# mLSTM cell and leaky-ReLU block: q of the second chunk's steps in own buffer parts, asked for sooner, and copied out of PSUM by VectorE

## Chip, cores and metric

The kernel runs on one core of a Trainium2 chip. The metric is device time in microseconds, the median of several executions.

## What is computed

Two blocks follow each other. The first is an mLSTM cell over 4 batches, 8 heads, 768 time steps and a head dimension of 40; the second a matmul, a leaky ReLU and a matmul over the 3072 tokens that come out. Cut to what matters:

```python
for t in range(S):
    m_new = np.maximum(f_gate[:, :, t] + m, i_gate[:, :, t])
    f_stab = np.exp(f_gate[:, :, t] + m - m_new)
    i_stab = np.exp(i_gate[:, :, t] - m_new)
    C = f_stab * C + i_stab * einsum('bhd,bhe->bhde', vt, kt)
    n = f_stab * n + i_stab * kt
    h = einsum('bhde,bhe->bhd', C, qt)
    y[:, :, t] = sigmoid(o_gate[:, :, t]) * h / np.maximum(np.abs(n @ qt), 1.0)
x = y.transpose(0, 2, 1, 3).reshape(B * S, H * D)      # 3072 x 320
h = x @ w_in                                           # 320 x 2048
out = np.maximum(0.01 * h, h) @ w_out                  # 2048 x 320
```

## The kernel before

**Steps and chunks.** Time is cut into 6 chunks of 128 (`NB`), and a chunk has one step per batch, so there are 24 steps; step s is chunk `s // 4`, batch `s % 4`. `B` is 4. Within a step the cell is worked out in parallel over its 128 times: scores of k against q, weighted by exponentials of the gates, times v, plus the state that the step inherits. Steps 0 to 3 (first chunk) are written out by hand in `first_chunk`. Steps 4 to 7 (second chunk) transpose k and q on TensorE; steps from 8 on load k and q in blocks of 32 and transpose them on VectorE (`prep_kq`). The feed-forward block of a chunk (`ff_units`) runs beside the cell steps of the next one: matmuls `ph` with w_in (L790), leaky ReLU on ScalarE (L798), matmuls `po` with w_out (L825), a copy (L833) and the store.

**Buffers for q.** `rb_t` holds `NR` = 2 buffers of three parts each: part 0 is for k in blocks (from step 8 on), part 1 for q, part 2 for the output gate. `natural(s, i)` (L396) gives part i of buffer `s % 2` for the steps 4 to 7. Part 0 of both buffers is not used by these four steps, whose k goes to `kn`. So q of steps 4 and 6 share one place, and q of 5 and 7 the other.

**A step of the second chunk.** `u_split(s)` (L554) transposes k and q of the step, 8 heads, two halves of 64 times: 64 small matmuls against the identity into two PSUM banks `tk`, each of which gets one half's k on some partitions and q on others. Four copies (L570) then take them to `kqT` in SBUF, k of both halves first, then q of both. `prep_qs(s)` (L512) has GpSimd scale q by a gate into a tile named `y`. `u_parts(s)` (L628) first transposes that scaled q on TensorE into two banks `tq` (L550), copied by ScalarE (L552); then come the scores (L644) and the state's increments (L649), and VectorE multiplies scores and exponentials (L654). `u_plain(s)` (L686) makes `hN` from them (L695), the denominators and the gated output x; `u_x(s)` (L763) transposes x into `xT`, the input of the next chunk's feed-forward matmuls, by five copies per step on ScalarE (L775 to L779). `prep_exp` (L481) makes the exponentials on ScalarE (L488), after GpSimd has added the mask (`prep_mask`, L479). `gates(c)` prepares the gates of a chunk on VectorE.

**Weights.** They arrive as 64-bit numbers and are narrowed on the core: `load_weights(n)` fetches a block, `narrow_weights(n)` yields six instructions, three on ScalarE (L243, L245, L251) and three on VectorE (L247, L253, L257). There are 4 blocks of w_in and 8 of w_out. The narrowing of two w_in blocks and of all w_out blocks lies among the cell steps of the second chunk. `fetch` says at which unit of the loop the later w_out blocks are asked for; the last one (7) at unit 15.

**Order.** For TensorE, VectorE, ScalarE and GpSimd the order of the instructions is the order in which the code gives them (`manual_schedule`, L989), and each engine works strictly in its order. SyncE issues nearly all transfers into one queue; its order is not written out but set by the framework's scheduler when the kernel is built, from the order of the code and from what each transfer depends on. `ahead(s)` (L868) prepares a step: `u_split`, the exponentials, `prep_qs`, and the requests for k and q of step s + 2; `feed(s)` (L890) asks for k and v of a step and for the spread gates `w` (L437). In the second chunk the loop at L1016 runs the feed-forward units of the first chunk one by one, and puts cell units behind those whose numbers `place` lists.

Of the kernel before, what the change touches and what calls it, by code (L numbers as in the profile page):

```python
# [21 lines left out]
def kernel(  # L22
# [26 lines left out]
    nc = tc.nc  # L49
    B, H, S, D = q.shape  # L50
# [12 lines left out]
    SL = P // 2  # L63
# [57 lines left out]
    NR = 2  # L121
# [5 lines left out]
    rb_t = [consts.tile([P, 3, RW], F32, name=f"rb{n}") for n in range(NR)]  # L127
# [57 lines left out]
    def run_of(r, at):  # L185

        ks = SLOTS[r][at:]
        return ks[0], next((i for i in range(1, len(ks)) if ks[i] != ks[i - 1] + 2), len(ks))

    def load_weights(n, halves=(0, 1)):  # L190

        m = n - QN
        if n < QN:
            dst = w_in[:, n, :]
        else:
            dst = w_out[:, 2 * m : 2 * m + 2, :].rearrange("p a d -> p (a d)")
        to = dst
        if wide:
            if n < 2:
                at = NF * GT - 2 * WC * (n + 1)  # L200
                raw = acts_l[:, at : at + 2 * WC].bitcast(U64)
            elif n < QN:
                raw = raw_t[:, WC * (n - 2) : WC * (n - 1)]
            elif m < 2:
                raw = w_out[:].rearrange("p f d -> p (f d)")[:, (2 + m) * WC : (3 + m) * WC].bitcast(U64)
            else:
                at = (4, 0, 1, 2, 3, 4)[m - 2] * HW
                raw = raw_t[:, at : at + HW]
            raws[n] = (raw, dst)
            to = raw  # L210
        if n < QN:
            src = moe_w_in[:, n * QC : (n + 1) * QC].rearrange("(k p) (r c) -> r p k c", p=DP, r=2)
            by_slot = to.rearrange("p (k c) -> p k c", k=KC)
            by_half = to.rearrange("p (e k c) -> p e k c", e=2, c=P)
            for r in halves:
                at = 0
                while at < KC:
                    k0, many = run_of(r, at)
                    rows, ks = slice(DP * r, DP * (r + 1)), slice(k0, k0 + 2 * many - 1, 2)
                    eng = nc.gpsimd if r and n < 3 else nc.sync  # L220
                    if wide or n > 1:
                        eng.dma_start(by_slot[rows, at : at + many, :], src[r, :, ks, :])
                    else:
                        for e in range(2):
                            eng.dma_start(by_half[rows, e, at : at + many, :], src[r, :, ks, e * P : (e + 1) * P])
                    at += many
        else:
            rows = moe_w_out[2 * m * P : 2 * (m + 1) * P, :]
            nc.sync.dma_start(to.rearrange("p (a d) -> p a d", d=Dm), rows.rearrange("(a p) d -> p a d", p=P))
# [165 lines left out]

    def natural(s, i):  # L396

        t = rb_t[s % NR][:, i]
        return t[:, : H * D].rearrange("p (h d) -> p h d", d=D)

    def load_late(s, i):

        if B <= s < 2 * B:
            if i > 0:
                c, b = divmod(s, B)
                nc.sync.dma_start(natural(s, i), (k, q, o_gate)[i][b, :, ts(c, P), :].rearrange("h p d -> p h d"))
        elif s < NS:
            load_blocks(s, i)
# [145 lines left out]
    def u_split(s):  # L554

        d = st[s]
        d["kqT"] = wk.tile([P, 2, PR * P], F32, name="kqT")
        src = (d["k"], natural(s, 1))
        bank = [psc.tile([P, H, SL], F32, name=f"tk{r}", tag="c") for r in range(2)]
        for h in range(H):  # L560
            for i in range(2):
                for u, toks, rows in subs(s):
                    out_rows = rows if i == 0 else slice(SL * u, SL * u + D)
                    nc.tensor.matmul(  # L564
                        bank[u][out_rows, h, :], lhsT=src[i][toks, h, :D], rhs=ident[toks, toks], start=True, stop=True,
                    )
        for i in range(2):
            for u, toks, rows in subs(s):
                out_rows = rows if i == 0 else slice(SL * u, SL * u + D)
                nc.scalar.copy(d["kqT"][rows, i].rearrange("p (h t) -> p h t", t=SL), bank[u][out_rows])  # L570

    def u_transpose(s, copy=nc.scalar.copy):
        d = st[s]
# [294 lines left out]
    def ahead(s):  # L868

        if s < NS:  # L870
            if s < 2 * B:
                u_split(s)
            if s >= 2 * B:
                late[s] = 3
            lazy[s] = prep_exp(s)
            if s < 2 * B:
                prep_qs(s)
            else:
                prep_kq(s)
            if s + NR < NS:  # L880
                load_late(s + NR, 0)
                load_late(s + NR, 1)
                if s + NR >= 2 * B:
                    spread_q(s + NR)
            state_next(s, 0)
            prep_vu(s)
            if s + 1 <= 2 * B:
                prep_mask(s + 1)

    def feed(s):  # L890
        load(s)
        spread(s)
# [96 lines left out]
    with tc.manual_schedule(engines={E.PE, E.DVE, E.Activation, E.Pool}):  # L989
        ffs, part = first_chunk()  # L990
        for s in (B, B + 1):
            load_late(s, 1)
            feed(s)
            load_late(s, 2)
            load_weights(s - B + 2)
        for n in range(3):
            load_weights(QN + n)
        for s in (B + 2, B + 3):
            feed(s)


        ffs = ffs[2:]
        fetch = {5: (3, 4), 8: (5, 6), 15: (7,)}
        place = (2, 5, 7, 10, 12, 15, 16, 18, 21, 22, 24, 26, 28)
        late = {}
        masks = {0: (2, 3), 12: (4, 5)}
        pairs = (2, 2, 6, 6, 14, 14, 19, 19, 19)
        now = (None for n in range(2, QN + NF // 2) for _ in narrow_weights(n))
        for c in range(1, NB + 1):
            if c > 1:  # L1010
                ffs = ff_units(c - 1)
            cells = cell_units(c) if c < NB else []
            n_ff, n_c = len(ffs), len(cells)
            done = fed = 0
            waiting = []
            for i in range(n_ff):  # L1016
                if c == 1:
                    run(now, (0, 0, 0, 3, 3, 0)[i] if i < 6 else 3 if i < 14 else 4)
                    for n in fetch.get(i, ()):
                        load_weights(QN + n)  # L1020
                for s, steps in lazy.items():
                    if s in late and late[s] > 0:
                        late[s] -= 1
                    else:
                        run(steps, 3)
                for n in masks.get(i, ()) if 1 < c < NB else ():
                    if c * B + n < NS:
                        prep_mask(c * B + n)
                ffs[i]()
                if c == 1 and i == 0:  # L1030
                    run(part)
                    prep_mask(B)
                    ahead(B)
                    load_fi(3)
                if c + 1 < NB:
                    if i == (1 if c == 1 else 0):
                        gates(c + 1)
                    if i == (3 if c == 1 else 2):
                        gates_exp(c + 1)
                upto = min(n_c, sum(p <= i for p in (place if c == 1 else pairs)))  # L1040
                while done < upto:
                    fn, s = cells[done]
                    fn(s)
                    done += 1
                    if fn is u_mix:
                        waiting.append(s)
                    if fn is u_plain and s < 2 * B - 1 or fn is u_parts and s == 2 * B - 1:
                        ahead(s + 1)
                    elif fn is u_mix:
                        ahead(s + 2)  # L1050
                    elif fn is u_plain:
                        prep_mask(s + 2)
                        ahead(s + 2)
                if i >= n_ff // 2 - 1:
                    for s in waiting:
                        gather_x(s)
                    waiting.clear()
                while fed < done:
                    fn, s = cells[fed]
                    fed += 1  # L1060
                    if fn in (u_mix, u_plain):
                        load_late(s + NR, 2)
                        if s + NL < NS:
                            feed(s + NL)
# [31 lines left out]
```

## Time and profile before

| | |
|---|---|
| median of 3 runs | 527.08 us (526.78 to 527.77) |
| the profiled execution's own time | 524.4 us |
| its span | 522.5 us |
| TensorE busy | 509.1 us (97%) |
| VectorE, ScalarE, GpSimd busy | 205.3, 187.6, 106.9 us |
| moved by DMA | 59.12 MB, mean 113 GB/s |

The profiled execution is one run under the hardware profiler; times of single instructions below are from it, counted from the start of its span. A row of a timeline gives start, duration, engine, line, operation, tiles and shapes; brackets give the idle time just before and what ended it. SPq is SyncE's row of transfers: its duration is that of the issue, not of the transfer. The copies of L570 are 16, of 577 to 583 ns, the first at 47.5 and the last at 101.2 us.

### The profile page before, as it was taken

What the parts mean: (1) busy time and instruction counts of PE and PEld (TensorE: products, weight loads), DVE (VectorE), ACT (ScalarE), POOL (GpSimd) and SP (SyncE); (2) the same over time, 40 slices, a digit from 0 to 9 for tenths busy, and PEclk for the clock granted to TensorE, in tenths of its full rate; (3) what the DMA queues carried; (4) which work ended last, traced back from release to release, by engine and by line L of the source; (5) the groups of instructions that cost most, each with busy time, mean ns of one, the idle gap of its engine ahead of it and who ended that gap; (6) DMA issues with size and microseconds to landing.
All of it is one profiled execution on the core that took longest, in us unless ns stands there. A gap on an engine that the chain in (4) does not pass through costs nothing.

```text
span 522.5 us, 11302 instructions
## 1 busy us (share of the span) xinstructions
PE 509.1 (97%) x4507; PEld 331.1 (63%) x4507; DVE 205.3 (39%) x400; ACT 187.6 (36%) x477; POOL 106.9 (20%) x149
## 2 busy tenths in 40 slices
PE   8989987999999999999999999999999999999997
PEld 6878876777554677554677554677554677544674
DVE  6666453767048264048264038253037240000000
ACT  5559896858425122125112125112125100122100
POOL 4363313424015031016021016021013010000000
PEclk9889999999999999999999999999999999999999
DMA  9999875989646535665536665625532112000000
GB/s 122 137 206 156 180 188 145 220 196 169 159 92 135 127 80 148 141 140 125 123 93 155 139 140 116 134 82 157 136 77 71 44 40 87 14 0 1 13 13 25
DMA packets 164419, 59.12 MB, mean 113 GB/s; under 512 B 128432, under 2 KB 155632, under 8 KB 164368
## 3 DMA queue, kind: packets, MB, share of 16 engines
q1 hardware_dynamic: 163408, 56.31, 50.1%
q0 software_dynamic: 576, 1.97, 2.0%
q8 instruction: 35, 0.57, 0.5%
q10 hardware_dynamic: 384, 0.13, 0.1%
q14 instruction: 16, 0.13, 0.1%
HBM read 51.68 MB, written 6.70 MB: 112 GB/s over the span
## 4 chain that ended last, share of the span: by engine, by line
PE 89%; SPq 5%; DMA 2%; ACT 2%; issue 1%; DVE 1%; ACTq 0%; DVEq 0%
PE po L825 40%; PE ph L790 39%; SPq L378 3%; PE pT L725 3%; PE sd L644 3%; DMA acts<-in_moe_w_in_dram 1%; PE sd L649 1%; PE tk L564 1%; PE hN L695 1%; DMA rb<-in_q_dram 1%; PE tq L550 1%; SPq L383 0%; SPq L392 0%; ACT kqT L570 0%; PE tg L357 0%
## 5 line engine op out<-in xcount | busy, mean ns | idle before, releaser
L790 PE MATMUL ph<-xT,w_in 64*128 64x512 f32 (+1 forms) x1120 | 216.5, 537 | 3.5 <-ACT acts L798 1.9
L825 PE MATMUL po<-w_out,acts 128*128 128x320 f32 x768 | 211.1, 434 | 0.0
L825 PEld LDWEIGHTS po<-w_out,acts 128*128 128x128 f32 x768 | 144.5, 190 | 62.6 <-issue 3.8
L790 PEld LDWEIGHTS ph<-xT,w_in 64*128 64x128 f32 x1120 | 108.6, 189 | 97.5 <-issue 87.7
L798 ACT ACTIVATE acts<-ph 128x512 f32<-128x512 f32 (+1 forms) x112 | 53.6, 531 | 141.5 <-PE ph L790 141.5
L654 DVE TENSOR_TENSOR qn<-w,sd 64x512 f32<-64x512 f32 x40 | 27.4, 684 | 106.7 <-PE sd L649 58.6
L479 POOL TENSOR_TENSOR w<-w,i 128x512 f32<-128x512 f32 x20 | 27.3, 1375 | 126.0 <-DMA w<-a_dr 74.0
L622 POOL TENSOR_TENSOR S<-S,f 40x336 f32<-40x336 f32 x36 | 28.0, 779 | 102.1 <-PE pT L725 65.2
L488 ACT ACTIVATE w<-w,gT 128x64 f32<-128x64 f32 x160 | 41.2, 338 | 0.0
L833 ACT COPY y<-po 128x320 f32<-128x320 f32 x12 | 5.1, 422 | 83.2 <-PE po L825 83.2
L833 ACT COPY hn<-po 128x320 f32<-128x320 f32 x12 | 5.1, 425 | 75.7 <-PE po L825 75.7
L541 DVE TENSOR_TENSOR qn<-kqT,ea 64x512 f32<-64x512 f32 x32 | 26.9, 840 | 0.9
L732 DVE STREAM_TRANSPOSE hb<-pT 128x512 f32<-128x512 f32 x16 | 11.4, 714 | 39.2 <-PE pT L725 39.0
L739 POOL TENSOR_TENSOR xb<-xb,den 128x320 f32<-128x320 f32 x16 | 11.6, 727 | 67.1 <-DVE xb L736 67.1
L644 PEld LDWEIGHTS sd<-kqT 40*64 40x64 f32 x640 | 19.9, 135 | 6.1 <-issue 6.1
L644 PE MATMUL sd<-kqT 40*64 40x64 f32 x640 | 21.6, 220 | 0.0
L535 DVE STREAM_TRANSPOSE kqT<-rb 128x512 f32<-128x512 f32 x32 | 20.7, 686 | 1.2 <-DMA rb<-in_q_dram 1.1
L743 DVE STREAM_TRANSPOSE x<-xb 128x512 f32<-128x512 f32 x16 | 18.1, 1132 | 7.7 <-POOL xb L739 7.7
L649 PE MATMUL sd<-S,vu 64*40 64x42 f32 x576 | 20.2, 214 | 0.7 <-issue 0.7
L649 PEld LDWEIGHTS sd<-S,vu 64*40 64x40 f32 x576 | 18.6, 111 | 0.9 <-issue 0.9
L626 DVE TENSOR_TENSOR S<-S,sd 40x336 f32<-40x336 f32 x36 | 18.1, 503 | 1.0
L725 PEld LDWEIGHTS pT<-qn,S 128*64 128x64 f32 x512 | 15.6, 138 | 3.6 <-issue 3.5
(138 smaller groups left out, 348.9 us busy)
## 6 DMA issues: line engine op xcount, KB each, us to landing
w<-a_dr SPq DMA_DIRECT2D x40, 128.0 KB
rb<-in_k_dram SPq DMA_DIRECT2D x64, 80.0 KB
rb<-in_q_dram SPq DMA_DIRECT2D x64, 80.0 KB
rb<-in_o_gate_dram SPq DMA_DIRECT2D x64, 80.0 KB
ea<-a_dr SPq DMA_DIRECT2D x32, 128.0 KB
kn<-in_k_dram SPq DMA_DIRECT2D x24, 160.0 KB
raw<-in_moe_w_out_dram SPq DMA_DIRECT2D x6, 640.0 KB
S<-in_v_dram SPq DMA_DIRECT2D x80, 40.0 KB
```

The source lines that it names most:

```text
L479: nc.gpsimd.tensor_tensor(w, w, cm2.unsqueeze(1).to_broadcast([P, H, SL]), op=ALU.add)
L488: yield nc.scalar.activation(w[:, h, :], of, AF.Exp, bias=gT[c][:, 0, bh : bh + 1], scale=1.0)
L535: nc.vector.transpose(d["kqT"][:, i].rearrange("p (h t n) -> p h n t", n=TS, t=QW), raw_blocks(s, i, QW).rearrange("p (h n) d -> p h n d", ...
L541: nc.vector.tensor_tensor(mixed(s)[rows, 1 - r], d["kqT"][rows, 1].rearrange("p (h t) -> p h t", t=SL), d["ea"][rows], op=ALU.mult,)
L622: nc.gpsimd.tensor_tensor(new, old, g, op=ALU.mult)
L644: nc.tensor.matmul(bank[1 - u][toks, h, :], lhsT=kqT[rows, 0, ts(h, SL)], rhs=kqT[rows, 1, ts(h, SL)], start=True, stop=True,)
L649: nc.tensor.matmul(dC[u][:, h].rearrange("p k d -> p (k d)"), lhsT=d["ku"][toks, h], rhs=S_v[s % NL][toks, u, h, :, :V1], start=True, stop ...
L654: nc.vector.tensor_tensor(mixed(s)[toks, u], w[toks], bank[1 - u][toks], op=ALU.mult)
L725: nc.tensor.matmul(pT[DP * r : DP * (r + 1), j * P + u * SL : j * P + (u + 1) * SL], lhsT=S[:, u, h, :], rhs=m[:, u, h, :], start=True, st ...
L790: nc.tensor.matmul(ph[r][:, cols], lhsT=w_row(r, slot, j), rhs=xT[DP * r : DP * (r + 1), slot, cols], start=(slot == 0), stop=(slot == KC ...
L798: nc.scalar.activation(acts[:, f, cols], ph[r][:, cols], AF.Prelu, alpha=0.01)
L825: nc.tensor.matmul(po[n][:], lhsT=acts[:, f, ts(n, P)], rhs=w_out[:, f, :], start=(f == 0), stop=(f == NF - 1),)
```

## The change

Three things change, all for steps 4 to 7.

1. `natural(s, 1)` gives part 0 of the buffer for steps 4 and 5, and part 1 as before for steps 6 and 7. Each of the four steps then has its own place for q. Part 0 is next written by k in blocks of steps 8 and 9.
2. `ahead(4)` and `ahead(5)` no longer ask for q of steps 6 and 7. These are asked for ahead of the loop: q of step 6 before the first three w_out blocks, q of step 7 between the two feeds of steps 6 and 7.
3. In `u_split` the two q copies out of PSUM go to VectorE; the two k copies stay on ScalarE.

```diff
     def natural(s, i):
 
-        t = rb_t[s % NR][:, i]
+        t = rb_t[s % NR][:, 0 if i == 1 and s < B + NR else i]
...
                 out_rows = rows if i == 0 else slice(SL * u, SL * u + D)
-                nc.scalar.copy(d["kqT"][rows, i].rearrange("p (h t) -> p h t", t=SL), bank[u][out_rows])
+                (nc.vector.tensor_copy if i else nc.scalar.copy)(
+                    d["kqT"][rows, i].rearrange("p (h t) -> p h t", t=SL), bank[u][out_rows],
+                )
...
                 load_late(s + NR, 0)
-                load_late(s + NR, 1)
+                if s + NR >= 2 * B:
+                    load_late(s + NR, 1)
...
             load_late(s, 2)
             load_weights(s - B + 2)
+        load_late(B + 2, 1)
         for n in range(3):
             load_weights(QN + n)
-        for s in (B + 2, B + 3):
-            feed(s)
-
+        feed(B + 2)
+        load_late(B + 3, 1)
+        feed(B + 3)
```

## Prediction

> **What bounds the kernel now.** I read the busy slices of the page first, then the table of waits, then the timelines of the engines around the waits that concern q. The slices:
>
> ```profile
> span 522.5 us, 11302 instructions
> PE   8989987999999999999999999999999999999997
> ACT  5559896858425122125112125112125100122100
> ```
>
> One slice is 13.1 us. TensorE is full from slice 7 on (from about 91 us), so what it is given earlier there can shorten the run. Its idle time lies before: in slice 6 (78 to 91 us) both TensorE and ScalarE dip. The waits name it:
>
> ```profile
> PE tk L564 <- DMA rb<-in_q_dram: 2.9, 1, 2.9
> POOL y L517 <- DMA rb<-in_q_dram: 1.3, 1, 1.3
> ```
>
> tk is the transposing of `u_split`, y the scaled q of `prep_qs`; one step waits for its q. TensorE's timeline says which, and SyncE's why:
>
> ```profile
> 79.56 0.31 PE L564 MATMUL tk<-ident,kn 64*40 64x64 f32 x4
> 82.75 0.25 PE L564 MATMUL tk<-ident,rb 64*40 64x64 f32 x2 [2.88 <-DMA rb<-in_q_dram]
> ```
> ```profile
> 58.84 1.12 SPq L229 DMA_DIRECT2D w_out<-in_moe_w_out_dram  x2
> 61.02 11.76 SPq L383 DMA_DIRECT2D S<-in_v_dram  x4
> 79.62 0.53 SPq L406 DMA_DIRECT2D rb<-in_q_dram  x1
> 114.45 0.54 SPq L229 DMA_DIRECT2D raw<-in_moe_w_out_dram  x1
> ```
>
> This is step 6 (third of the second chunk). Its q is issued at 79.62, behind everything that SyncE fetched for steps 6 and 7, and lands 3.1 us later. Four v issues take 11.76 us, where four elsewhere take about 2.5: they stand in a full queue. The DMA share is 0.89 from 58 to 75 us.
>
> ScalarE sets the pace up to there, and is itself held by transfers twice:
>
> ```profile
> 62.24 2.37 ACT L570 COPY kqT<-tk 40x512 f32<-40x512 f32 x4 [0.88 <-PE tk L564]
> 65.13 1.38 ACT L243 ACTIVATE w_in<-raw 128x1280 f32<-128x1280 f32 x1 [0.53 <-DMA raw<-in_moe_w_in_dram]
> 119.87 0.79 ACT L243 ACTIVATE w_out<-raw 128x640 f32<-128x640 f32 x1 [8.13 <-DMA raw<-in_moe_w_out_dram]
> 132.88 0.42 ACT L833 COPY hn<-po 128x320 f32<-128x320 f32 x1 [0.54 <-PE po L825]
> 133.21 0.37 ACT L775 COPY xT<-xt 128x256 f32<-128x256 f32 x1
> ```
>
> Remember 119.87: the last weight block arrives there, and from there ScalarE works without a pause to 132.34. At the seam between the chunks the weight load of the next matmuls was waiting for ScalarE too:
>
> ```profile
> PEld ph L790 <- ACT xT L779: 0.4, 1, 0.4
> ```
> ```profile
> 133.17 2.16 PE po L825 x8
> 135.33 4.91 PE ph L790 x21
> ```
>
> [...]
>
> **The change, part by part.**
>
> *q of step 6 asked for sooner.* Steps 4 and 5 now read q from part 0 of their buffers, so steps 6 and 7 own part 1, and their q has nothing to wait for. In the built program SyncE issues q of step 6 straight behind the four loads of the last w_in block (the last begins at 58.19), before the w_out blocks. That w_in block lands at 65.1 (ScalarE starts on it at 65.13). A q is 160 KB in runs of 160 bytes. The k of step 6, of the same form, landed at 72.0, after the last w_out block before it had come nearly whole at 70.1 (arrivals of the DMA semaphores in the trace): some 1.0 to 1.9 us; I take 1.2. So q is there at about 66.5, 13 us before it is read. The step's transposing took 79.56 to 83.84, 4.28 us; step 7's took 1.12. Gain on TensorE: 4.28 - 1.12 = 3.16 us.
>
> *Does TensorE get to 79.56 sooner?* No. Before it stand ScalarE's activations, and these run on from 65.13 without a pause to 79.9. All that the change takes off ScalarE before that (steps 4 and 5, 2.3 us, with it TensorE's 0.75 us wait at 57.40) ends in a longer wait for that w_in block. Credit: 0.
>
> *q of step 7 asked for sooner.* Issued at 94.33, it landed at 98.23, and TensorE read it at 98.24: no wait, and no slack. With TensorE 3.16 us ahead it would have become a wait of about 3 us. Now it is issued before k of step 7, around 76 us. Worth nothing by itself, it keeps the gain.
>
> *The q copies on VectorE.* 8 copies leave ScalarE, each 0.580 us: 4.6 us. Nearest row for VectorE: L581, 128x512 out of PSUM, 0.671 us: 8 x 0.67 = 5.4 us, on an engine 39% busy. The end of a step's copies: before, 4 x 0.58 = 2.32 us after tk; now 0.58 + 0.58 + 0.67 = 1.83 us, since the second bank's k copy goes first. Between 1.83 and 2.6 us (all in series with hand-overs) nobody is late: scores are 4.5 us of ph matmuls or more behind tk. VectorE's waiting copy blocks what is queued behind it, mostly weight narrowing (L253, L257); in step 6 that is wanted by po at 92.68 - 3.2 = 89.5 and would be done by about 84. In step 4 `gates` starts 1.3 us later and ends at 53.2, before the scores' product (54.27 before, then limited by ScalarE at about 53.1). At nothing; without that cover at most 0.6 us a step.
>
> *The DMA queue.* No transfer is added. q of step 6 pushes the three w_out blocks, and k, v and w of step 6, back by about 1.2 us, q of step 7 those of step 7 by 0.6 more. First use: w_out at 73.87, in by 66.6 before, so 67.8 now. w of step 6: POOL's mask (L479) began at 76.88, as w came; now about 78.1, over at 79.4, in time for POOL's next work at 79.76. Later two issues (0.6 us each) are missing from the row, at 79.62 and 94.33[...]. So the last weight block, issued at 114.45, should come within -0.6 to +0.8 us of 119.85; I take 0 and call the shift D.
>
> *What is late next.* All of SyncE's waits between 61 and 119 us on compute are under 1.3 us, so an earlier TensorE doesn't bring that block sooner. Thus ScalarE starts on it at 119.87 + D as before, and its row of work is unchanged: 12.47 us without a pause to 132.34, then the hn copy (0.33 to the next start; its wait of 0.54 is gone, po being early), then the first xT copy of step 7 (0.35): 133.02 + D. TensorE, 3.16 ahead, ends po at 135.33 - 3.16 = 132.17, and its next matmuls need that copy. In the built program the first waits for the copies up to L777 (the changed kernel's number) alone, the slots after for the rest, which come sooner than they are reached. So the second chunk's ph begins at 133.02 + D against 135.33: **2.3 us sooner**, 0.85 us of the gain turned into a new wait there. po's last quarter needs the block narrowed: 123.43 + D against 126.05 + 1.07 - 3.16 = 123.96, just in time.
>
> From there TensorE is full to the end and the shift stays. Sum: 3.16 - 0.85 = 2.3. The profiled execution: 524.4 (span 522.5 and 1.9 around it) to 522.1. The median of the runs shown, 527.08, stands 2.7 above it; I take the same gain off: **524.8**.
>
> **The rivals.**
>
> *Main case* (0.53): as worked out, D between -0.6 and 0.8: gain 1.5 to 2.9, 524.2 to 525.6.
>
> *The whole gain stays* (0.20): the last block comes 0.85 us or more sooner, or ScalarE's row is shorter. For: DMAs leave full stretches of the queue. Against: no reason that it be that much. 3.16 us: 523.9.
>
> *Much given back at the seam* (0.21): D is 0.8 to 3.3, or the first matmul waits for all five xT copies (134.3: gain 1.0), or hN of step 7 (112.3 for TensorE; its inputs were ready at 111.67) waits too. For: the wait of 8.13 shows that this block is the late one. Gain about 0.9: 526.2. With D at 2.3 the change does nothing.
>
> *Slower* (0.06): the early q, in short runs, holds up the big w_out blocks and all behind them, so that the last block slips by more than the whole gain and 0.2% more. It decides from D = 2.3 + 1.05 = 3.4; at D = 4, 528.8. Against: D would have to be about three times a q's service. That the change doesn't do what it says is excluded by the built order, except that a wait for k, v or w of step 6 may replace that for q: k moves from 72.0 to 73.2, far from 79.56.
>
> **How the numbers follow.** About 0.2% (1.05 us) is what a measurement here can tell from no change. Faster by more than that: the first two cases and a small part of the third, 0.77; within: 0.17; slower: 0.06. The range leaves out the low gains of the third case, the slower one and a sliver at the top: gain 0.8 to 3.4, 523.7 to 526.3.
>
> **What would show it.** Right: no wait of tk for q; tk of step 6 begins at about 79.6 and takes 1.1; L570 shows 8 copies on ScalarE, 8 on VectorE near 0.6 to 0.67; ScalarE's wait for the last w_out block grows beyond 8.1 us and ends near 119.9; a new wait of about 0.9 of ph for xT near 132 to 133. Wrong: that block landing more than 1.5 us from 119.9, tk of step 6 well after 79.6, or a wait of sd or hN for VectorE's copies.

## The result, and the profile after

The changed kernel took 528.01 us (median of 21 runs), the kernel before 526.70 us (21 runs on the same chips in turn): ratio 1.0019, 95% interval 1.0000 to 1.0039. A gain is excluded; what is left lies between nothing and a loss of 0.4%. The forecast was 524.8 us, and the time lies outside its range. A few runs in a slower state, such as one of these 21 (532.8 us) and one of o_n_after's five below (592.6 us), are left out of the ratios.

The profiled execution of the changed kernel took 527.76 us (span 525.6), close to its median. That of the kernel before, 524.4 us, was 2.3 us better than its median, so the two traces differ by more (3.1 us of span) than the medians do (1.3 us).

From the start of the third chunk's stage on, both kernels run alike. The second chunk's ph matmuls begin at 135.25 us before and at 138.34 after, and from there to the end of the span it is 387.25 and 387.26 us. So the whole difference of the two traces is made before that seam, and one view of that stretch is enough. The waits of TensorE after, from 40 to 145 us (total, how many, longest):

```profile
PE tg L352 <- DVE hn L708: 4.7, 1, 4.7
PE ph L792 <- ACT acts L800: 2.1, 2, 1.1
PE tk L564 <- ACT acts L800: 0.7, 1, 0.7
```

The wait of tk for q (2.9 us before) is gone. A new one stands in the list, longer than the old: tg, the transposes of the next chunk's gates (`gates_T`, L352), waits for hn, the gated output of step 6. TensorE's row shows where:

```profile
93.94 0.25 PE L564 MATMUL tk<-ident,kn 64*40 64x64 f32 x2
...
94.97 2.42 PE L827 MATMUL po<-w_out,acts 128*128 128x320 f32 x8
102.04 0.39 PE L352 MATMUL tg<-ident,bu 32*128 32x32 f32 x2 [4.65 <-DVE hn L708]
```

TensorE is done with po at 97.39, and stands till 102.04. Before, it came to tg at 101.65 and went on at once. It now arrives 4.3 us sooner and leaves 0.4 us later. The rows of ScalarE and VectorE say what hn waited for:

```profile
96.81 0.79 ACT L243 ACTIVATE w_out<-raw 128x640 f32<-128x640 f32 x1 [7.68 <-DMA raw<-in_moe_w_out_dram]
...
100.94 0.44 ACT L524 ACTIVATE rb<-rb 128x320 f32<-128x320 f32 x1
```
```profile
97.63 0.49 DVE L247 TENSOR_SCALAR w_out<-w_out 128x640 f32<-128x640 f32 x1 [6.89 <-ACT w_out L243]
...
101.41 0.49 DVE L708 SCALAR_TENSOR_TENSOR hn<-rb,hN 128x320 f32<-128x320 f32 x1 [0.55 <-ACT rb L524]
```

Read it from the end. hn (L708) needs the tanh of step 6's output gate, L524 on ScalarE. This is ready only at 101.38, because in ScalarE's order it stands behind the narrowing of two w_out blocks, and the first of these blocks (number 3; the other is 4) arrived at 96.8. ScalarE had stood for 7.68 us in front of it, VectorE for 6.89. tg itself has nothing to do with these weights or with hn: its PSUM place is that of step 6's hN, which hn is the last to read.

In the kernel before, the same narrowing began at 94.35, hn was done at 99.52 and tg came at 101.65, without a wait:

```profile
94.35 0.81 ACT L243 ACTIVATE w_out<-raw 128x640 f32<-128x640 f32 x1
99.03 0.49 DVE L706 SCALAR_TENSOR_TENSOR hn<-rb,hN 128x320 f32<-128x320 f32 x1
101.65 0.31 PE L352 MATMUL tg<-ident,bu 32*128 32x32 f32 x2
```

The slack that I never looked for was 2.1 us.

What the change was to do to the copies, it did. Its group view gives count, and shortest, median and longest duration in ns:

```profile
L570 ACT COPY kqT<-tk x8: 578/580/581, 45.3 to 102.0; 40x512 f32<-40x512 f32 x8
L570 DVE COPY kqT<-tk x8: 683/688/693, 46.2 to 103.2; 40x512 f32<-40x512 f32 x8
```

**Half clock.** The stall has a second price. Four stretches of the changed kernel by engine (the three columns at the end are the granted TensorE clock, the DMA engines' share and GB/s), and then the same 16 po matmuls behind tg, after and before:

```profile
98.00:102.00 4.00, 0.00 (x0) 0.00 (x0) 2.44 (x8) 3.89 (x6) 0.00 (x0) 0.86 0.68 117
102.00:104.00 2.00, 1.96 (x8) 1.73 (x9) 1.91 (x4) 1.99 (x5) 1.88 (x3) 0.50 1.09 262
104.00:108.00 4.00, 4.00 (x10) 2.55 (x9) 3.57 (x5) 0.08 (x1) 2.71 (x4) 0.54 1.09 331
108.00:112.00 4.00, 4.00 (x105) 3.10 (x104) 0.99 (x2) 2.54 (x4) 1.39 (x2) 1.00 0.57 110
```
```profile
103.22 6.78 PE L827 MATMUL po<-w_out,acts 128*128 128x320 f32 x16
```
```profile
102.33 4.57 PE L825 MATMUL po<-w_out,acts 128*128 128x320 f32 x16
```

In windows of 0.1 us the granted clock of the changed kernel is 0.50 from 100.9 to 107.6 us, 0.81 and 0.55 in the two at the edges, and 1.00 in all others from 78 to 136: one stretch at half clock, from about 100.9 to 107.7 us (in the kernel before the clock is 1.00 in all four). It begins 3.5 us after TensorE stopped and 1.2 us before it goes on. TensorE looks just as busy in it, but works at half speed for 5.65 us and so loses 2.8 us. The timelines agree: from the start of tg to the end of these 16 matmuls it is 7.96 us after and 5.25 before, 2.7 us more.

### The profile page after: what moved, and what is told of

It is laid out like the page before. It is cut to its first block, busy times and chain, and to the rows that moved or that the text cites. A ratio compares the mean times of both kernels' runs of the same rounds, so it can differ in the third digit from the quotient of the medians.

```text
span 525.6 us, 11300 instructions
## 1 busy us (share of the span) xinstructions
PE 510.8 (97%) x4507; PEld 333.8 (64%) x4507; DVE 209.6 (40%) x408; ACT 182.5 (35%) x469; POOL 107.1 (20%) x149
## 4 chain that ended last, share of the span: by engine, by line
PE 80%; SPq 2%; ACT 0%; DMA 0%; issue 0%; DVE 0%; ACTq 0%
PE po L827 39%; PE ph L792 33%; PE pT L727 3%; PE sd L646 3%; SPq L383 1%; PE sd L651 1%; PE tg L357 0%; DMA S<-in_v_dram 0%; SPq L422 0%; PE tg L352 0%; PE hN L697 0%; PE tq L550 0%; ACT raw L245 0%; PE xt L774 0%; ACT w_out L243 0%
## 5 line engine op out<-in xcount | busy, mean ns | idle before, releaser
L827 PE MATMUL po<-w_out,acts 128*128 128x320 f32 x768 | 213.3, 438 | 0.0
L827 PEld LDWEIGHTS po<-w_out,acts 128*128 128x128 f32 x768 | 146.0, 192 | 63.3 <-issue 5.4
```

The lines of the kernel that those rows point to most:

```text
L827: nc.tensor.matmul(po[n][:], lhsT=acts[:, f, ts(n, P)], rhs=w_out[:, f, :], start=(f == 0), stop=(f == NF - 1),)
```

## The experiments

All times are medians; ratios are against the kernel before, which ran beside each.

### The two parts alone: a_requests, b_copies

a_requests is the changed kernel with all copies on ScalarE (L570: `nc.scalar.copy(` again). b_copies is the kernel before with this in place of its `nc.scalar.copy(`:

```diff
+                (nc.vector.tensor_copy if i else nc.scalar.copy)(
```

> The changed kernel with all four copies of kqT left on ScalarE: own parts for q and early requests alone. Theory 1 (the weights' transfers hold the end of the second chunk): tk no longer waits for q, but TensorE waits 3 to 5 us at the gate transposes tg, since ScalarE's tanh for step 6 stands behind the narrowing of w_out blocks that have not arrived; time 526.5 to 528.5, like before and after. Theory 2 (the copies on VectorE, with the swapped order of w_out blocks 5 and 6 that the built program shows with them, eat the gain): 524 to 525, over 1.5 us faster than before.

> The kernel before with the two q copies of each step on VectorE: copies alone. Theory 1: tk of step 6 still waits about 3 us for q; time as before within 0.5 us. Theory 2: slower than before by 1 us or more, with ScalarE's wait for w_out block 5 longer by about 2.5 us, because block 6 is fetched ahead of it in the built program.

a_requests: 528.96 us, 1.0031 (1.0012 to 1.0051). b_copies: 527.27 us, 1.0006 (0.9981 to 1.0032). The requests alone carry the result, with the same wait (tg for hn, 4.9 us), half a microsecond above theory 1's range; the copies, and the swapped order of blocks 5 and 6 that comes with them, are worth nothing that can be measured. The same pair also shows what becomes late: in the three kernels with q asked for early (the changed one, a_requests, and g_after below) ScalarE starts on the first of the blocks at 96.8, 98.2 and 97.9 us after waits of about 7 us; in three without (before, b_copies, g_before) at 94.4, 93.9 and 94.8 with at most 0.1 us of wait.

### No late blocks: n_after, n_before

Both kernels without the transfers of w_out blocks 3 to 7. Their narrowing stays and works on old words, so these parts of w_out are not the true ones.

```diff
-            nc.sync.dma_start(to.rearrange(...), rows.rearrange(...))
+            if m < 3:
+                nc.sync.dma_start(to.rearrange(...), rows.rearrange(...))
```

> The changed kernel without fetching w_out blocks 3 to 7 (their narrowing works on what stands in the buffer, so the second matmul's result is wrong from there). Theory 1: with the queue relieved no wait at tg, no stretch at half clock, and the whole gain of about 3.2 us shows against the same kernel made from before: 523 to 524. Theory 2: no better than the kernel before without these fetches.

> The kernel before without fetching w_out blocks 3 to 7 (as in the run beside it, the second matmul's result is wrong). Both theories: tk of step 6 still waits for q, about 3 us, since that q is issued before these blocks; time within 0.7 us of before. It is the base for the run beside it.

526.47 us (0.9987, 0.9968 to 1.0005) and 526.73 us (0.9987, 0.9966 to 1.0009): 0.3 us apart, where my theory asked for 3. So the blocks alone were not it. The waits of n_after show why:

```profile
PE tg L353 <- DVE hn L709: 2.4, 1, 2.4
...
ACT rb L525 <- DMA rb<-in_o_gate_dram: 5.3, 1, 5.3
```

tg still waits for hn, now because the output gate of step 6 itself comes late: its request stands at 96.45 in SyncE's row, and it lands at 100.0. The mean granted clock of the span is 0.983 in n_after and 0.990 in n_before, so the clock may have taken its part again; how much of that lies behind this wait is not shown.

### tg out of the way: g_after, g_before

`u_gates` one unit earlier, so that tg comes before the work of step 6:

```diff
-            units.insert(2 * B - 2, (u_gates, c + 1))
+            units.insert(2 * B - 3, (u_gates, c + 1))
...
-        place = (2, 5, 7, 10, 12, 15, 16, 18, 21, 22, 24, 26, 28)
+        place = (2, 5, 7, 10, 12, 14, 15, 18, 21, 22, 24, 26, 28)
```

> The changed kernel with the gate transposes tg (L352) one unit of the loop earlier, ahead of the work of step 6 whose gated output hn they waited for. Theory 1 (the 3 us won at tk of step 6 are taken back by tg's wait for hn, and the half clock behind that wait costs up to 3.4 us more): the wait of 4.7 us and the half-clock stretch behind it are gone; what is late next is the last w_out block (about 124 us), with ScalarE's row behind it, so the next chunk begins at about 137 instead of 138.3; 1 to 3 us faster than the changed kernel, 525 to 527. Theory 2 (the last w_out block and ScalarE's row behind it alone set the end of the stage): the next chunk still begins at about 138, the stall only moves to the seam; 528, as the changed kernel. Theory 3 (TensorE then stalls at step 6's own next operand by as much): another wait of 3 us or more at hN or xt, 527 to 528.

> The kernel before with the same move of the gate transposes, as a control. All theories: q's wait of 2.9 us at tk of step 6 stays, tg did not wait in this kernel, so nothing changes: 526.7 within 0.7. If it is faster by over 1 us, the place of the gate transposes matters by itself, and g_after says nothing about the change.

526.66 us (0.9978, 0.9954 to 1.0003) and 526.68 us (0.9991, 0.9972 to 1.0009). Against the changed kernel's 528.0 this is some 1.3 us, but against its own control it is nothing. The time lies in theory 1's range, but the trace is of theory 3's kind, at an operand that no theory named: the stall moves on to the next that stands behind the same block, here the tk of step 7, whose PSUM place is freed by a VectorE copy that is queued behind the narrowing.

```profile
PE tk L564 <- DVE f L364: 3.1, 1, 3.1
```

Behind it TensorE is slower, which theory 1 did not have: a single po matmul takes 0.83 us at 100.66, where one ahead of the wait took 0.43 (94.79); in the changed kernel one at a granted clock of 0.50 took 0.90 (103.22).

### The blocks from GpSimd's queue: p_after, p_before

g_after and g_before, with w_out blocks 3 to 7 asked for by GpSimd:

```diff
+            eng = nc.sync if m < 3 else nc.gpsimd
...
+        fetch = {8: (3, 4), 11: (5, 6), 15: (7,)}
```

> g_after, and w_out blocks 3 to 7 asked for from GpSimd's queue, in the loop's units 8, 11 and 15, so that they stand in no queue of SyncE's. Theory 1: with neither tg's wait nor a late last block, the 3 us won at q stay to the end of the stage, and no half-clock stretch comes: 522 to 524.5. Theory 2: the last block comes sooner, and with it the end of the stage; also 522 to 525, but then g_after shows no gain. Theory 3: 526 or more, with a wait at another operand of the cell steps.

> g_before, and w_out blocks 3 to 7 asked for from GpSimd's queue as in p_after. q's wait at tk of step 6 stays, since q stands behind other transfers of SyncE's. Theory 1: 525.5 to 527, so that p_after is about 3 us below it. Theory 2: the earlier blocks shorten the stage as much here as in p_after: both within 1 us of each other.

529.54 us (1.0035, 1.0015 to 1.0055) and 532.83 us (1.0097, 1.0061 to 1.0133). Blocks 3 and 4 came at 86.6 and 89.4 us, but the transfers of SyncE's row came later for it: the output gate of step 6 landed at 108.0 in p_after, and q of step 6 cost a wait of 7.3 us in p_before. In p_after the late output gate held up GpSimd, and TensorE waited 4.0 us for its scaled q (L551), as its theory 3 has it. p_before is far above theory 1's 527, and not within 1 us of p_after as in theory 2. Here, moving the requests moved the delay.

### Six kernels that tell nothing of the question: no_after, no_before, f_after, fa_after, s_after, s_before

The first two put the output gates of steps 6 and 7 into places of the raw buffer and asked for them ahead of the loop; the next two asked for blocks 3 to 7 earlier (`fetch = {2: (3, 4), 5: (5, 6), 13: (7,)}`), fa_after also for the output gates from ScalarE.

> n_after (the changed kernel without the transfers of w_out blocks 3 to 7), and the output gates of steps 6 and 7 in unused places of the weights' raw buffer, asked for ahead of the loop, so that neither a block nor an output gate can arrive late. Leaves out the true values of those blocks. Theory A (the 3 us won at q were eaten by the next late arrivals, first the blocks, behind them the output gate of step 6, each of which had only 0 to 2 us of slack): no wait of tg for hn of step 6, no half-clock stretch near 102, 3 us or more below no_before: 522 to 524. Theory B (ScalarE's or VectorE's row of work in the stage sets the time, whatever arrives): another wait of TensorE of 2 us or more before 135, within 1 us of no_before.

> n_before with the output gates of steps 6 and 7 placed and asked for as in no_after; q is asked for as in the kernel before. Control: q's wait of about 3 us at tk of step 6 stays; 526 to 527 in both theories.

> The changed kernel with w_out blocks 3 to 7 asked for 2 or 3 units of the loop sooner; in the built program blocks 3 and 4 stand some ten transfers further ahead in SyncE's row, and the output gate of step 6 some places nearer to them. Theory A: the blocks land 4 to 6 us sooner, the wait at tg falls to that for the output gate (2.4 us in n_after); the last block lands sooner than 124 too; 525.5 to 527, 1 to 2.5 us below the changed kernel. Theory B: 527.5 to 528.5, as the changed kernel.

> f_after, with the output gates of steps 6 and 7 asked for by ScalarE instead of SyncE, so that they don't stand in SyncE's row (each costs ScalarE an issue). Theory A: output gate 6 lands by about 92 to 96, the wait at tg is gone or below 1 us, no half-clock stretch near 102; 522.5 to 525. Theory B: within 1 us of f_after.

552.36, 550.98, 555.19 and 555.62 us. In the order of the code the places were still those of w_in blocks that were not yet narrowed. The narrowing therefore took the new transfer's words for its own (that part of the computation is changed) and waited for them; no_before:

```profile
ACT w_in L244 <- DMA raw<-in_o_gate_dram: 29.2, 1, 29.2
```

s_after and s_before have all work in place, and ask for blocks 3 and 4 and the two output gates from ScalarE:

```diff
+                eng = nc.scalar if i == 2 and s >= B + NR else nc.sync
...
+            eng = nc.scalar if m in (3, 4) else nc.sync
...
+        fetch = {7: (3, 4), 8: (5, 6), 15: (7,)}
```

> The changed kernel with w_out blocks 3 and 4 and the output gates of steps 6 and 7 asked for by ScalarE at the first places in its row where the buffers are free, so that they don't stand in SyncE's row; nothing is left out. Theory A: blocks 3 and 4 land by about 91 and the output gate of step 6 by about 88, the wait of tg for hn is gone or below 1 us with the half-clock stretch behind it, 2.5 to 5 us below the changed kernel: 523 to 525.5; unless the last w_out block (124) then stalls the end of the stage, which would leave 1.5. Theory B: within 1 us of the changed kernel.

> The kernel before with the same requests moved to ScalarE. Theory A: q's wait stays (2 to 4 us, a little less if SyncE's row gets shorter ahead of q), so 525.5 to 527 and 1.5 us or more above s_after. Theory B: as s_after, within 1 us.

551.87 and 547.43 us. ScalarE's row of s_after:

```profile
60.95 1.18 ACT L572 COPY kqT<-tk 40x512 f32<-40x512 f32 x2 [0.92 <-PE tk L566]
94.94 0.40 ACTq L408 DMA_DIRECT2D rb<-in_o_gate_dram  x1
95.51 1.35 ACT L244 ACTIVATE w_in<-raw 128x1280 f32<-128x1280 f32 x1 [33.38 <-DMA ea<-a_dr]
```

ScalarE stands 33 us in front of its own request. In the built program this request carries a wait on a completion semaphore that SyncE's transfers also use: the one counted before it there is a transfer (ea) that SyncE asks for at 91.17 us and that completes at 94.86. Here a request moved to another engine brought its place in the first engine's order along.

### Neither late: o_n_after, o_n_before, o_n_requests

n_after and n_before again, with the output gates of steps 6 and 7 in the raw-buffer places of blocks 3 and 4, asked for where those blocks were (unit 5, when the places are free). Left out is the same as in n_after; blocks 3 and 4 are narrowed from another place.

```diff
+                    if i == 5:
+                        load_late(B + 2, 2)
+                        load_late(B + 3, 2)
```

> n_after (the changed kernel without the transfers of w_out blocks 3 to 7), and the output gates of steps 6 and 7 in the raw-buffer places of blocks 3 and 4, asked for where these blocks were. Leaves out the true values of those blocks; the narrowing of blocks 3 and 4 is done on another place. Theory A (the 3 us won at q were eaten by the next late arrivals: the blocks first, behind them the output gate of step 6, each with 0 to 2 us of slack): with neither of them late tg of step 6 has no wait for hn and no half-clock stretch follows; 2.5 to 4 us below o_n_before: 522 to 524. Theory B (ScalarE's or VectorE's row of work in the stage sets the time, whatever arrives): another wait of TensorE of 2 us or more before the next chunk, within 1 us of o_n_before.

> n_before with the output gates of steps 6 and 7 placed and asked for as in o_n_after; q is asked for as in the kernel before. Control: q's wait of about 3 us at tk of step 6 stays; 526 to 527 in both theories.

> o_n_after with all four copies of a step out of PSUM on ScalarE again, so that of the change only the buffer parts and the requests are left (as before, the true values of w_out blocks 3 to 7 are left out). Theory A (late arrivals ate the gain, the copies' engine is worth nothing either way): as o_n_after, 521 to 523.5, 3.5 us or more below o_n_before, with no wait of TensorE of over 1 us between 75 and 135. If the copies on VectorE carry part of the gain once nothing arrives late: 523.5 to 526, with a wait of TensorE behind ScalarE.

o_n_after: 521.99 us, 0.9895 (0.9865 to 0.9926, four runs). o_n_before: 526.58 us, 0.9992 (0.9974 to 1.0010). o_n_requests, which has the requests of the change and not its copies: 522.58 us, 0.9906 (0.9874 to 0.9937). o_n_requests ran on another chip than the pair, so its ratio is the better measure. With nothing late behind it the early q is worth 4.0 to 4.6 us by the medians and 4.5 to 5.1 by the ratios, and again the copies' engine makes no difference that shows. The trace shown is that of o_n_requests. TensorE's waits there from 40 to 145 us, and its row:

```profile
PE ph L795 <- ACT acts L803: 1.4, 2, 1.1
PE sd L654 <- issue: 0.9, 1, 0.9
PE sd L654 <- POOL vu L511: 0.4, 1, 0.4
```
```profile
94.28 2.42 PE L830 MATMUL po<-w_out,acts 128*128 128x320 f32 x8
96.64 0.31 PE L353 MATMUL tg<-ident,bu 32*128 32x32 f32 x2
```

tg comes at 96.64 without a wait, the clock stays at 1.00 in every stretch from 78 to 136 us, and the third chunk's stage begins at 130.24, against 139.46 in o_n_before (a slower execution than its median, 529.6 us, while that of o_n_requests, 519.5, was its fastest).

### The same with all the work: e_after

The changed kernel, with blocks 3 and 4 and the output gate of step 6 asked for by GpSimd:

```diff
+            eng = nc.gpsimd if m in (3, 4) else nc.sync
...
+                eng = nc.gpsimd if i == 2 and s == B + NR else nc.sync
...
+        fetch = {7: (3, 4), 8: (5, 6), 15: (7,)}
...
+                    if i == 7:
+                        load_late(B + NR, 2)
```

> The changed kernel with w_out blocks 3 and 4 and the output gate of step 6 asked for by GpSimd at the loop's unit 7, behind its mask for step 6 (about 80 us); nothing is left out, the other requests stay in SyncE's row. Costs GpSimd three issues of about 0.75 us ahead of its work for step 6. Theory A (late arrivals of the blocks and then of the output gate ate the 3 us): blocks land by about 90, the output gate by about 91 (before: 93.8, 96.8 and 98.1), tg's wait for hn and the half clock behind it are gone, and 2.5 to 5 us come back against the changed kernel's 528: 523 to 525.5. If the last w_out block still comes at 124, a wait of 1 to 2 us at the seam of the chunks takes part of it: 525. Theory B (the engines' own work sets the time): 527 to 528.5. A miss by another way: a wait of over 2 us for scaled q or for k of steps 6 or 7, because GpSimd or the second queue delays them.

529.87 us, 1.0058 (1.0033 to 1.0083), above both theories. The 0.75 us for an issue of GpSimd were an estimate; in the changed kernel's trace two of its issues take 1.39 us (L222, at 12.95) and two 1.25 (at 25.84). These transfers came as early as hoped (87.6, 89.7 and 91.0 us), hn of step 6 was done at about 99.9, and tg's wait and the half clock behind it were gone (the granted clock is 1.00 in every stretch from 78 to 112 us). But SyncE's row slipped, and the next two blocks were the late ones:

```profile
113.57 0.78 ACT L244 ACTIVATE w_out<-raw 128x640 f32<-128x640 f32 x1 [10.93 <-DMA raw<-in_moe_w_out_dram]
...
124.63 0.79 ACT L244 ACTIVATE w_out<-raw 128x640 f32<-128x640 f32 x1 [3.63 <-DMA raw<-in_moe_w_out_dram]
```
```profile
PE hN L699 <- DVE qn L658: 3.8, 1, 3.8
```

Step 7's hN now waits, and the granted clock is 0.85 from 112 to 124 us and 0.86 from 124 to 136, which is 3.5 us of full clock less. No version with the whole work was clearly faster than the kernel before: g_after's 0.9978 has an interval that ends at 1.0003.

## Why the prediction was wrong, step by step

**q of step 6 asked for sooner: right, and under-sized.** The wait is gone. I valued it at 3.16 us. The o_n kernels show 4.0 to 5.1, and a term that I left out is the clock: of the five traces that have q's wait at 2.9 to 3.5 us, four have a lower granted clock from 83.0 to 90.5 us (0.82 in b_copies, 0.77 in n_before, 0.78 in g_before, 0.77 in o_n_before). Of these 7.5 us that takes 1.4 to 1.7 us of full clock; 3.16 + 1.7 = 4.9, an estimate that has TensorE at work in all of the slow part. The one trace without (before, 1.00) is the one that I worked from. The full clock there may be part of the 2.3 us by which that execution beat its median; that isn't shown. That this q, issued behind the loads of the last w_in block, would not delay them was my assumption; in the trace ScalarE starts on that block at 64.21 us, before at 65.13.

**No earlier arrival at tk of step 6: right in kind.** Its start lies at 78.0 to 79.7 in before, after, a_requests and b_copies, in no order that the change explains; in the changed kernel's trace it is 1.1 us earlier than in that of the kernel before (78.5 and 79.6).

**q of step 7: right for q, wrong for what it passes.** TensorE read it at 93.94 without a wait. But it now stands ahead of w_out blocks 3 and 4, which before it followed. I priced that at 0.6 us for "those of step 7" and asked only when the last block would come.

**The copies on VectorE at nothing: right.** 8 x 0.69 us where I had 0.67. In step 6 the first q copy starts at 80.27, when ScalarE is done with k of the same bank (80.24); b_copies against before and o_n_after against o_n_requests give no difference that can be measured.

**The DMA queue, D between -0.6 and 0.8: wrong.** The last w_out block came at 124.0 us, so D was 4.1. ScalarE's three waits for blocks in the changed kernel sum to 20.1 us (7.7, 5.3, 7.1). Part of D comes from the blocks ahead of it: between 100 and 125 us SyncE itself waited 2.2 and 1.0 us for the completion of a w_out block (before: 1.2). My rival "slower" was priced at D = 4 with 528.8 us, near the result; but that is luck: in this trace the end of the stage wasn't set by that block. By the formula, 133.02 + 4.1, the seam would stand at 137.1; it came at 138.34, and no matmul waits there in either kernel.

**What is late next: this is the step that failed.** I wrote "What is late next" and answered with the last block alone, 40 us further on. Between 83 and 135 us I followed TensorE as if it could move 3.16 us forward in one piece. But tg had only 2.1 us of slack on hn. And hn, like everything behind the narrowing in ScalarE's and VectorE's order, was tied to blocks with little or no slack: in the trace before, block 3 arrived at 94.33 and ScalarE began on it at 94.35 (in g_before and b_copies it lay there for 0.9 and 1.5 us). The runs put in its place: a gain of 4.3 us on the way to tg (3.16 from q, 1.1 from the earlier start of step 6 in that execution), a stall of 4.65 us there, and 2.7 us lost to half clock. By the sum (-4.3 + 4.65 + 2.7) the seam comes 3.1 us later, as it does.

**What stays open.** Why the early q's make block 3 come later is split up only in part. It arrives at 96.8 to 98.2 us in the three traces with them, and at 92.4 to 94.3 in the three without. From the first request of the last w_in block to that of block 3, SyncE's row takes 33.0 to 33.8 us with them and 30.9 to 31.1 without. Some 2 us of this lie in the four v requests of step 7, which q of step 7 now stands before: 5.1 to 5.7 us against 3.1 to 3.2. The rest is service: from its request block 3 takes 8.4 to 8.6 us against 6.5 to 7.2, and why is not shown. That the late output gate takes the gain is shown by o_n against n, which both lack the blocks. That late blocks take it too is read from the traces of the changed kernel, g_after and e_after; no run leaves only the blocks late. That no order of SyncE's row could avoid it is not shown, since that order is the scheduler's and I didn't try one written by hand.

## What to carry to other kernels

When a stall is removed, move every later instruction of that engine forward by the gain and ask each of its waits, unstalled ones too, for its slack; a wait that doesn't appear in the profile because its operand comes 2 us early is the first to appear. On engines that work strictly in order (ScalarE stood 7.68 us in front of the narrowing, with the tanh behind it), the operand to check is not only the instruction's own: it is whatever late transfer stands ahead of its producer. And look up the granted clock behind a stall of TensorE, which can cost more than its length: the half clock added 2.7 us to the 4.65 us of tg's wait, and nothing to the 2.9 us of q's wait in the kernel before.

## What the runs showed of the hardware

Waits of TensorE and the granted clock behind them, in profiled executions. q's wait, with the clock from 83.0 to 90.5 us: 2.9 us, 1.00 (before); 2.9 us, 0.77 (n_before); 3.2 us, 0.78 (g_before) and 0.77 (o_n_before); 3.5 us, 0.82 (b_copies). tg's wait of 4.7 us in the changed kernel: 0.50 from 100.9 to 107.7 us. hN's wait of 3.8 us in e_after: 0.85 from 112 to 124 us, 0.86 from 124 to 136. In o_n_requests, with no wait above 1.1 us from 40 to 145 us, the clock is 1.00 in every stretch from 78 to 136. The length of the wait alone does not settle it: before and n_before both have 2.9 us. I had not reckoned with a lower clock for a wait of about 3 us.

Behind tk's wait of 3.1 us in g_after a single po matmul takes 0.83 us, ahead of it 0.43. Of four waits only the mean clock of the whole span is shown: 2.4 us, 0.983 (n_after); 4.9 us, 0.989 (a_requests); 4.0 us, 0.984 (p_after); 7.3 us, 0.986 (p_before). It can't be put down to the wait alone: the span of the kernel before has a mean of 0.992 with its clock at 0.50 from 19.6 to 23.1 and from 33.3 to 36.8 us, and at 1.00 from 40 us on.

Counted as half of the time that TensorE works in it (an estimate), the stretch of the changed kernel costs 2.8 us, and the timelines give 2.7. It is 6.8 us long and costs less than half of that, because its first 1.2 us fall into the wait.
